# All loads of x on one queue, and a new order of tasks, in a fused state-space and MLP kernel

## The chip, the cores and the metric

One core of a Trainium2 chip runs the whole program. The metric is the device time of one execution in microseconds (us), median of several runs. The profile is one further execution; its span runs from the first to the last instruction of the program.

## The reference, cut to what matters

All inputs are bf16; L = 2048 positions, D = P = 448 channels, F = 1792 hidden channels.

```python
xn = layernorm(x)                                   # over the 448 channels
# branch A: a diagonal complex recurrence over the 2048 positions
Lam = Lambda_re + 1j * Lambda_im ; dt = exp(log_dt) ; Lam_bar = exp(dt * Lam)
Bu  = xn @ (((Lam_bar - 1) / Lam)[:, None] * (B_re + 1j * B_im)).T
h_t = Lam_bar * h_{t-1} + Bu_t
s   = 2 * real(h @ (C_re + 1j * C_im).T) + xn * Dskip
# branch B: an MLP on the same rows
y   = gelu_tanh(layernorm(xn) @ w1 + b1) @ w2 + b2
out = x + s * silu(y)
```

## The kernel before, in words

The 2048 positions are cut into 8 blocks of 256 rows; partition p of a block holds its rows 2p and 2p+1 ("par" 0 and 1). Two blocks make a group g, and there are four groups. For each group the kernel normalises the rows (twice: `xn` for branch A, `xm` for branch B), transposes them (by DMA, in group 0's branch B by TensorE), and then

- mm1 (L789): `w1` times the transposed rows, 7 steps j of two hidden tiles each, every step in a first part of 6 matmuls and a second of 8, into one of three pairs of PSUM banks; a gelu on ScalarE (L793) empties the pair into `gT`. In group 0 this is done block by block with 256 columns, later with 512;
- mm2 (L814): 14 matmuls for each block and par, into bank 5 or 6 in turn; VectorE adds `b2bc` (L817, tile `o`), which frees the bank, and a silu follows (group 0 and 3 by ScalarE's Silu, L819; group 1 and 2 by Tanh, L821, and VectorE);
- Bu (L717): 14 or 7 matmuls into bank 4, emptied into `u_sb` (L404). VectorE turns `u` by the cosines and sines in `WT`, scans (L741), and turns back into `h_sb`;
- the output part (L857, L860, L863): `h_sb` times the scaled C, plus for par 0 a matrix `M0` that stands for what lies within a row pair.

`WT` and the small per-channel columns (`cw`, `ang`) are worked out at the start on VectorE, GpSimd and ScalarE. ScalarE loads a function table five times: exp and log at the start, gelu (L428), silu and sine (L609), gelu again (L613), silu at the end.

**Who does what, and when.** Every piece of work is a task, numbered in the order in which the program makes it. `link()` finds what each task must wait for; `emit()` then issues all 628 tasks in the list `ORDER`, so each engine, and each DMA queue, runs its own tasks in the order in which they stand there. `kb.either` gives a task two engines; the list `SECOND` names the tasks that take the second. SyncE (SP) issues nearly all DMAs; an engine's DMA issue waits in that engine's queue like any other task. Tasks that the text names by number:

| tasks | what |
|---|---|
| 21; 20, 19; 47 | loads of x: block 1; block 0's par 1 and par 0; blocks 2 and 3 |
| 16, 17, 18 | loads of the rows Lambda_re, Lambda_im, log dt |
| 22, 23; 27, 28; 30, 31; 33, 34 | the four chunks of `w1`, each in two DMAs |
| 24, 29, 32, 35 | a copy of 64 rows of each `w1` chunk to the other half (L349) |
| 95, 92, 100, 98 | row statistics of block 0 par 1, par 0, block 1 par 1, par 0 (L416) |
| 108, 104, 132, 129 | normalised rows of these (L438) |
| 109, 105, 133, 130; 111, 107, 134, 131 | their transposes on TensorE (L445), and the copies of these into `xn2T` (L404) |
| 112, 113 | the columns of b1 (L589), and their copy `b1f` (L592) |
| 103; 117, 120, ..., 140 | load of the gelu table (L428); group 0's gelus; 140 is the last that block 0 needs |
| 114, 115, 116 | first mm1 parts |
| 58 to 61 | angles: range reduction on GpSimd (59), ScalarE's absolute value (60), the sine polynomial (61) |
| 44; 45, 46 | broadcasts of b2 and of D to all partitions, issued by GpSimd; D halved |
| 173 to 178 | `ra`, `rb`: arguments of the sines (L621 to L626, tile `s_w`) |
| 275, 272, 281, 278 | mm2 of group 0, banks 6, 5, 6, 5; their b2 additions are 276, 273, 282, 279, their silus 277, 274, 283, 280 |
| 179; 180 to 184; 284 | load of the silu and sine table (L609); five sines into `WT` (L635); load of the gelu table (L613) |
| 285 to 305 | mm1 and gelus of group 1; 288, 294 are the first two gelus, 298 the matmuls that take the banks of 294 |
| 330, 334, 376; 331, 335 | Bu groups, and the copies of the banks of 330 and 334 |
| 370, 371, 373, 374; 474, 475, 477, 478 | normalised rows of groups 2 and 3 for branch B (L486 on VectorE, L487 on ScalarE) |

The b2 and D broadcasts as they stand:

```python
ld("pool", b2bc[:], ..., ["b2bc"], 114688, -50, reads=["sgn3", "w1r_3"])
ld("pool", dbc[:], ..., ["dbc"], 114688, -20, reads=["b2bc"])
```

`reads` makes the DMA wait for these: b2's for the last piece of `w1` (task 34), D's for b2's landing.

Of the kernel before, what the change touches and what calls it, by code (L numbers as in the profile page):

```python
# [13 lines left out]
PINNED = -1e5  # L14
# [146 lines left out]
20 14 1 0 19 10 95 21 22 15 17 92 96 16 18 25 93 5 23 28 98 97 26 108 3 94 104 27 2 48 91 49 30 50 66 51 4 109 111 6 105 100 99 101 31 106 112 107 102  # L161
110 114 113 115 24 56 116 57 132 119 52 118 53 55 129 29 32 67 9 47 130 34 44 103 120 131 133 117 54 134 122 12 33 58 124 123 121 127 171 156 135 42
252 169 165 40 125 128 137 126 35 141 136 7 43 172 170 253 8 143 68 173 138 59 13 174 251 256 254 163 144 258 60 142 146 176 257 166 147 139 255 61
259 260 148 41 206 151 140 164 152 154 145 205 149 153 175 63 207 150 45 263 64 155 275 38 36 62 70 179 177 69 261 276 72 178 215 262 264 272 265 193
71 277 273 180 168 181 281 194 182 219 46 75 65 160 73 74 183 191 249 76 282 77 78 80 274 86 167 197 278 285 192 158 279 79 195 283 289 198 208 196
184 190 209 287 201 362 286 37 211 250 363 293 82 85 366 367 361 290 210 81 11 217 365 39 218 364 368 216 269 187 280 369 161 188 284 288 199 266 267
292 200 294 291 83 87 298 296 185 202 297 302 162 303 295 301 299 270 300 89 322 323 304 370 373 374 324 305 203 213 212 360 310 271 204 159 214 223
221 84 224 306 325 222 189 225 359 227 268 157 226 330 186 228 229 307 311 314 231 375 341 90 230 232 331 88 441 336 233 220 234 334 235 337 335 326
327 371 237 376 236 338 377 372 312 342 339 238 241 239 328 329 340 378 332 343 379 380 344 313 308 318 345 381 347 333 382 242 240 245 356 352 243
442 383 246 244 357 247 404 465 467 351 358 346 353 354 468 405 348 385 406 408 407 412 413 472 466 355 309 411 248 409 349 417 410 421 471 384 386  # L170
387 388 350 414 415 422 469 470 416 425 319 320 398 443 426 427 389 420 418 428 429 390 423 473 419 433 315 424 451 430 434 444 463 445 392 436 474
399 477 446 447 504 316 400 478 401 496 437 391 393 402 403 480 431 505 475 435 481 317 479 506 507 497 321 432 483 484 482 508 438 509 488 439 510
489 448 476 485 511 464 499 491 492 455 500 440 532 536 513 512 514 515 394 534 533 449 395 490 450 396 540 486 502 537 397 535 452 539 493 541 501
526 545 543 516 549 538 544 542 519 521 548 546 518 551 498 550 456 566 457 517 520 527 528 522 529 453 454 567 458 530 459 487 568 531 569 590 460
461 591 552 523 524 570 525 571 593 547 494 462 592 575 495 594 574 576 580 572 557 558 573 598 577 553 599 554 595 579 582 555 601 578 596 581 503
585 586 587 583 588 556 589 563 602 603 597 559 600 560 584 564 611 608 604 605 561 612 562 565 613 606 609 616 620 610 614 607 624 617 615 618 621
619 625 622 623 626 627
""".split()]
SECOND = [int(k) for k in """
46 52 54 55 56 63 65 72 77 78 79 80 84 85 89 90 107 113 131 134 159 162 164 178 185 186 189 190 191 197 223 225 227 229 243 249 250 259 261 329 346  # L180
359 360 370 373 374 393 439 444 463 464 474 475 497 500 502 503 505 507 520 524 569 592 604 607
# [17 lines left out]
def bass_recurrent_scan__ssm_conv_s5__mixer_channel_mlp__prompt_kernel(  # L199
# [18 lines left out]
    with ExitStack() as es:  # L218
# [49 lines left out]
        De = s_w.bitcast(BF)[:, 1, 3, 0:512].rearrange("p (d c) -> p d c", d=4)  # L268
        h_sb = SB("h_sb", [128, 2, 7, NK + 2])
# [33 lines left out]
        with nc.Block():  # L303
# [29 lines left out]
            for i, vec in enumerate((A_Lambda_re, A_Lambda_im, A_log_dt)):  # L333
                ld("act", vrows[i:i + 1, 64:512], dram_ap(vec, 0, [[D, 1], [1, D]]), [f"vr{i}"], 1000, 10 * PINNED)
# [17 lines left out]
            for par in range(2):  # L352
                ld("sp" if par or not 1 else "act", x_all[:, 0, par, :], dram_ap(A_x, par * D, [[2 * D, 128], [1, D]]), [f"x0p{par}"], 114688, S1)
# [12 lines left out]
            ld("pool", b2bc[:], dram_ap(B_b2, 0, [[0, 128], [1, D]]), ["b2bc"], 114688, -50, reads=["sgn3", "w1r_3"])  # L366
            ld("pool", dbc[:], dram_ap(A_Dskip, 0, [[0, 128], [1, D]]), ["dbc"], 114688, -20, reads=["b2bc"])
# [16 lines left out]
            def ln_stats(g, prio, blocks=(0, 1)):  # L384
                for b in blocks:
                    for par in range(2):
                        q = par * 2 + b
                        dve([lambda e, b=b, par=par, q=q: e.bn_stats(lnst[:, q, :], x_all[:, 2 * g + b, par, :])], [f"x{2 * g + b}"] , [f"st{q}"], 0.62, prio)
                for b in blocks:
                    for par in range(2):  # L390
                        q = par * 2 + b
                        dve(lambda e, q=q: e.bn_aggr(lnmv[:, g % 2, q, :], lnst[:, q, :]), [f"st{q}"],
                            [f"mv{g % 2}_{q}"], 0.16, prio)
# [612 lines left out]
```

## Time and profile before

| | |
|---|---|
| median of 3 runs | 155.37 us (155.31 to 155.9) |
| the profiled execution | 155.16 us, of which the span is 153.4 us |
| granted TensorE clock | 0.998 |
| busy: PE, VectorE (DVE), ScalarE (ACT), GpSimd (POOL) | 148.9, 134.0, 91.4, 32.9 us |
| first mm1 matmul, first mm2 matmul, end of the last matmul | 7.41, 20.08, 150.5 us |

PE is TensorE's matmul row, PEld its weight loads, SP the queue of SyncE. A row of the timeline gives the start, the length, the engine, the line, the operation and, in brackets, the idle time before it and what ended it; successive rows of one line are merged. The granted clock is full throughout, so a matmul's length shows the work and not the throttle.

### The profile page before, as it was taken

The page shows a single profiled execution, that of the slowest core. Times are in us where ns is not written, and L with a number is a line of the kernel's source. Part 1 is how long each engine was busy: PE and PEld are TensorE (multiplying, and loading weights), DVE is VectorE, ACT ScalarE, POOL GpSimd, SP SyncE. Part 2 cuts the span into 40 slices and gives each one's busy share as a digit, 9 for nine tenths or more (in the row PEclk, how much of TensorE's full clock was granted, in tenths as well). Part 3 has the DMA queues.
Part 4 walks back from the last instruction along what each step waited for, and adds up shares of the span by engine and source line. Part 5 has one row for each costly group of instructions (what it writes and reads, how often), then busy time and mean ns, then how long its engine had stood idle before and what let it go on. Part 6 is the DMA issues. An engine that isn't in the chain of part 4 may idle for free.

```text
span 153.4 us, 2996 instructions
## 1 busy us (share of the span) xinstructions
PE 148.9 (97%) x1138; PEld 87.6 (57%) x1138; DVE 134.0 (87%) x297; ACT 91.4 (60%) x167; POOL 32.9 (21%) x87
## 2 busy tenths in 40 slices
PE   7999999999999999999999999999999999999992
PEld 7777755454565667654443556764554666555551
DVE  2959989899998899999989998849999848999994
ACT  3598897998871479868765940026389337418010
POOL 5105648133810000020145000022500006000200
PEclk9999999999999999999999999999999999999999
DMA  4899999899889923000003061311900001001022
GB/s 133 244 308 383 225 220 140 146 260 126 154 155 170 135 93 68 0 6 0 0 0 60 4 128 60 68 60 23 142 19 0 0 4 60 0 0 60 4 83 98
DMA packets 31236, 14.73 MB, mean 96 GB/s; under 512 B 24752, under 2 KB 30774, under 8 KB 31222
## 3 DMA queue, kind: packets, MB, share of 16 engines
q1 hardware_dynamic: 30768, 14.14, 41.5%
q0 software_dynamic: 160, 0.23, 0.9%
q8 instruction: 9, 0.15, 0.4%
q10 hardware_dynamic: 294, 0.17, 0.4%
q14 instruction: 5, 0.04, 0.1%
HBM read 6.89 MB, written 1.84 MB: 57 GB/s over the span
## 4 chain that ended last, share of the span: by engine, by line
PE 96%; DVE 1%; issue 0%; DVEq 0%
PE psum L789 29%; PE psum L814 28%; PE psum L717 14%; PE psum L857 12%; PE psum L860 4%; PE psum L407 3%; PE psum L706 3%; PE psum L445 1%; PE psum L863 1%; DVE t L871 1%; DVE tmp L877 0%; PE psum L692 0%; DVEq L303 0%; PE psum L589 0%; DVE ones L306 0%
## 5 line engine op out<-in xcount | busy, mean ns | idle before, releaser
L789 PE MATMUL psum<-xn2T,w_sb 64*128 64x512 bf16 (+1 forms) x462 | 45.5, 346 | 0.4
L814 PE MATMUL psum<-w_sb,gT 128*128 128x448 bf16 x224 | 44.2, 353 | 0.0
L793 ACT ACTIVATE gT<-psum,b1f 128x512 bf16<-128x512 f32 (+1 forms) x66 | 36.6, 622 | 11.0 <-PE psum L789 10.5
L789 PEld LDWEIGHTS psum<-xn2T,w_sb 64*128 64x128 bf16 x462 | 24.2, 110 | 20.6 <-issue 2.6
L814 PEld LDWEIGHTS psum<-w_sb,gT 128*128 128x128 bf16 x224 | 21.8, 98 | 19.7 <-issue 0.2
L717 PE MATMUL psum<-xnT,BT 128*128 128x256 bf16 x196 | 24.0, 273 | 0.0
L717 PEld LDWEIGHTS psum<-xnT,BT 128*128 128x128 bf16 x196 | 18.7, 98 | 5.4 <-issue 1.1
L404 ACT ACTIVATE u_sb<-psum 128x512 bf16<-128x512 f32 (+2 forms) x21 | 9.9, 472 | 18.1 <-PE psum L717 18.0
L741 DVE TENSOR_TENSOR_SCAN s_w<-dk,vs 128x774 f32<-128x774 f32 x8 | 14.1, 1763 | 0.1
L857 PE MATMUL psum<-CZ,h_sb 128*128 128x448 bf16 x56 | 11.9, 353 | 0.0
L817 DVE TENSOR_TENSOR o<-psum,b2bc 128x448 f32<-128x448 f32 x16 | 9.6, 609 | 1.6 <-PE psum L814 1.2
L857 PE MATMUL psum<-CQ,h_sb 128*128 128x448 bf16 (+2 forms) x54 | 10.5, 332 | 0.0
L404 ACT ACTIVATE vs<-s_w 64x256 bf16<-64x256 f32 (+2 forms) x9 | 6.9, 772 | 5.5 <-DVE s_w L741 5.2
L877 POOL TENSOR_TENSOR tmp<-t,x_all 128x448 bf16<-128x448 bf16 x3 | 3.1, 1034 | 32.4 <-DVE t L871 17.8
L486 DVE TENSOR_SCALAR xn_sb<-x_all,lnw 128x448 bf16<-128x448 bf16 (+2 forms) x28 | 9.5, 368 | 0.3
L653 ACT ACTIVATE tmp<-Cr,cw 128x448 f32<-128x448 bf16 (+1 forms) x11 | 7.2, 664 | 3.2 <-DVE CQ L656 3.1
L752 POOL TENSOR_TENSOR ang<-s_w,ang 128x16 f32<-128x16 f32 x3 | 1.6, 535 | 33.6 <-ACT s_w L750 33.6
L487 ACT ACTIVATE xn_sb<-x_all,lnw 128x448 bf16<-128x448 bf16 (+2 forms) x12 | 7.4, 648 | 2.1 <-DVE xn_sb L486 2.0
L857 PEld LDWEIGHTS psum<-CZ,h_sb 128*128 128x128 bf16 x56 | 5.3, 98 | 5.1 <-DVE Cr L869 0.4
L821 ACT ACTIVATE th<-o 128x448 f32<-128x448 f32 x8 | 4.6, 573 | 5.3 <-DVE o L817 5.3
L857 PEld LDWEIGHTS psum<-CQ,h_sb 128*128 128x128 bf16 x54 | 5.1, 98 | 4.1 <-DVE tmp L877 0.4
L860 PE MATMUL psum<-M,xnT 128*128 128x448 bf16 x32 | 7.4, 352 | 0.0
(161 smaller groups left out, 195.5 us busy)
## 6 DMA issues: line engine op xcount, KB each, us to landing
out_dram<-tmp SPq DMA_DIRECT2D x7, 224.0 KB, 1.9
x_all<-in_A_x_dram SPq DMA_DIRECT2D x3, 448.0 KB, 4.3
w_sb<-in_B_w_dram SPq DMA_DIRECT2D x3, 448.0 KB, 7.3
w_sb<-in_B_w_dram SPq DMA_DIRECT2D x3, 384.0 KB, 5.7
vs<-in_A_C_re_dram SPq DMA_DIRECT2D x1, 392.0 KB, 12.2
vs<-in_A_C_im_dram SPq DMA_DIRECT2D x1, 336.0 KB, 10.4
Bn<-in_A_B_im_dram SPq DMA_DIRECT2D x1, 336.0 KB, 10.8
Bn<-in_A_B_re_dram SPq DMA_DIRECT2D x1, 336.0 KB, 10.9
```

Source lines behind the costliest of these rows:

```text
L404: kb.either(("act", [lambda e, o=o, i=i: e.activation(o, i, ACT.Copy) for o, i in pairs]), ("dve", [lambda e, o=o, i=i: e.tensor_copy(o, i ...
L486: on = [("dve", [lambda e, o=o, i=i: e.tensor_scalar(o, i, rs, nb, op0=ALU.mult, op1=ALU.add) for o, i in parts], 0.4, 0.12), ("act", [lam ...
L487: ("act", [lambda e, o=o, i=i: e.activation(o, i, ACT.Identity, bias=nb, scale=rs) for o, i in parts], 0.75, 0.2)]
L653: on = [("act", [lambda e, o=o, i=i, c=c: e.activation(tmp[o, k, :], b[i], ACT.Copy, scale=c[i]) for o, i, c in ps], 0.66 * len(ps), 0.2), ...
L717: fns = [lambda e, r=r, m=m, d=d: e.matmul(psum[:, 4, r * NK:(r + 1) * NK], BT[:, m, d, :], xnT[:, gx, d, :], start=(d == 0), stop=(d == 6 ...
L741: dve(lambda e, so=so, vi=vi: e.tensor_tensor_scan(so, dk[:].rearrange("p i c -> p (i c)"), vi, 0.0, ALU.mult, ALU.add), ["v", "vl", "dk", ...
L789: return lambda e: e.matmul(view(bk[k]), w1_sb[rows, d, fcol(2 * j + k)], rhs[rows, d, :, :], start=not second and n == 0, stop=second and ...
L793: act([lambda e, k=k: e.activation(gT[:, gb, 2 * j + k, :].rearrange("p (r c) -> p r c", r=2)[:, :, cols], view(bk[k]), ACT.Gelu_apprx_tan ...
L814: fns = [lambda e, fi=fi: e.matmul(psum[:, bk, 0:D], gT[:, gb, fi, q * 128:(q + 1) * 128], w2_sb[:, fi, :], start=(fi == 0), stop=(fi == N ...
L817: dve(lambda e: e.tensor_tensor(o2[:, fb, :], psum[:, bk, 0:D], b2bc[:], ALU.add), [f"ps{bk}", "b2bc"], [f"oo{fb}"], 0.62, prio - 76)
L857: fns = [lambda e, k=k: e.matmul(psum[:, bk, c0:c1], h_sb[:, hb, k, k0:k0 + 128], cm[:, k, c0:c1], start=(k == 0), stop=False) for k in ra ...
L860: fns += [lambda e, d=d: e.matmul(psum[:, bk, c0:c1], xnT[:, gx, d, xs], M0[:, d, c0:c1], start=False, stop=(d == 3)) for d in range(4)]
```

## The change

Four edits, with flags in the source set so that other new branches (`if 0`, `0 >> g & 1`) do nothing.

1. Block 0's par 0 (task 19) is loaded by SP and no longer by ACT, and the row log dt (task 18) too. With the new order SP issues: block 1 of x, block 0 par 1, block 0 par 0, log dt, then `w1`.
2. D's broadcast (45) waits for what b2's waits for, and no longer for b2's landing. Both stay on GpSimd's queue.
3. `ORDER` is new: all 628 tasks are there in another order.
4. `SECOND` is new. By it 19 tasks go from DVE to ACT, 12 from ACT to DVE, 26 from POOL to DVE, 18 from DVE to POOL. Among those that go to ACT are 24, 35, 46, 113, and the branch B rows 370, 373, 374, 474, 475; 164, 191, 197, 444, 477 and 500 go from ACT to DVE. No task is added or dropped, and no shape changes.

```diff
-20 14 1 0 19 10 95 21 22 15 17 92 96 16 18 25 93 5 23 28 98 97 26 108 3 94 104 27 2 48 91 49 30 50 66 51 4 109 111 6 105 100 99 101 31 106 112 107 102
...
+10 21 1 2 17 20 0 26 100 16 95 14 25 19 92 18 15 3 6 22 96 23 93 27 101 28 48 5 97 91 30 49 98 94 108 50 112 109 99 51 104 106 102 105 111 132 67 52
+53 24 107 56 110 133 114 55 54 113 129 134 66 68 115 31 4 116 29 57 11 58 130 119 118 103 171 117 131 47 169 32 9 121 170 33 120 122 59 34 60 124 43
+156 61 125 13 251 123 252 254 42 63 165 163 253 257 255 258 256 259 41 126 260 127 40 135 172 128 137 173 141 35 157 136 138 62 143 139 207 144 177
+206 205 142 158 38 148 72 175 8 146 263 140 152 145 69 147 261 149 166 70 71 151 153 44 154 7 159 262 174 275 150 36 64 155 215 45 272 46 276 264 176
+164 75 178 265 161 273 168 191 73 249 219 74 179 281 193 194 76 278 192 277 167 65 274 180 220 39 282 285 195 279 85 181 182 77 196 362 283 366 183
...
-                ld("act", vrows[i:i + 1, 64:512], dram_ap(vec, 0, [[D, 1], [1, D]]), [f"vr{i}"], 1000, 10 * PINNED)
+                ld("sp" if 1 and i == 2 else "act", vrows[i:i + 1, 64:512], dram_ap(vec, 0, [[D, 1], [1, D]]), [f"vr{i}"], 1000, 10 * PINNED)
...
-                ld("sp" if par or not 1 else "act", x_all[:, 0, par, :], dram_ap(A_x, par * D, [[2 * D, 128], [1, D]]), [f"x0p{par}"], 114688, S1)
+                ld("sp" if par or not 0 else "act", x_all[:, 0, par, :], dram_ap(A_x, par * D, [[2 * D, 128], [1, D]]), [f"x0p{par}"], 114688, S1)
...
-            ld("pool", dbc[:], dram_ap(A_Dskip, 0, [[0, 128], [1, D]]), ["dbc"], 114688, -20, reads=["b2bc"])
+            ld(("pool", "sp")[0], dbc[:], dram_ap(A_Dskip, 0, [[0, 128], [1, D]]), ["dbc"], 114688, -20, reads=[] if 0 else ["sgn3", "w1r_3"])
```

The tasks named below stand, per engine, as follows in the new order (before `|` after):

```
DVE  95 92 96 93 98 108 104 100 99 101 107 113 24  |  100 95 92 96 93 101 98 108 99 104 132 67 53 107
ACT  111 102 57 103 120 117 ...                     |  102 111 24 113 57 103 117 120 ...
ACT  155 179 261 277 180 181 182 183 191 274 197 283 184 280 284  |  155 46 179 277 274 180 181 182 283 183 184 280 284
POOL 67 9 44 12 58 7 8 68 59 13 61 45               |  58 9 59 61 13 63 158 72 8 44 7 45
PE   109 105 106 112 110 114                        |  112 109 106 105 110 133 114
```

## The prediction

> **What bounds the kernel now.** I read the page first, then the chain that ended last in order of time, then busy time by stage, then the timelines of the first 36 us and the DMA view.
>
> ```profile
> PE 148.9 (97%) x1138; PEld 87.6 (57%) x1138; DVE 134.0 (87%) x297; ACT 91.4 (60%) x167; POOL 32.9 (21%) x87
> ...
> PE 96%; DVE 1%; issue 0%; DVEq 0%
> ```
> TensorE is the bound and the chain hardly leaves it. From the first mm2 (20.08) to the last output group (149.78) it runs almost without a hole: adding each group at its quickest spacing in this trace (mm2 2.65 us, Bu 1.52 or 0.76, mm1 parts 0.645 and 0.865, output 2.08 and 1.32) gives 126.96 of these 129.70 us. Of the 2.74 us left, about 1.6 are a tenth at each change from mm1 to another kind, which any order pays; some 1.1 are real waits. So a new order can win about 1 us behind 20.08, and can lose without limit.
>
> ```profile
> 0.00:7.41 7.41, 6.22 (x66) 5.36 (x67) 4.32 (x15) 3.56 (x10) 2.83 (x14) 1.00 0.67 186
> 7.41:20.08 12.67, 12.42 (x178) 9.29 (x177) 10.55 (x41) 10.86 (x24) 5.65 (x22) 1.00 1.08 297
> 20.08:30.78 10.70, 10.70 (x58) 5.39 (x57) 9.66 (x34) 9.64 (x18) 4.82 (x15) 1.00 0.94 166
> ```
> Columns: window, length, busy PE, PEld, DVE, ACT, POOL, clock, DMA share, GB/s. In 7.41 to 20.08 PE looks busy, but its mm1 matmuls are spread (68 take 5.14 us, 76 ns each, where the first 28 take 1.65, 59 each): they wait for banks that ScalarE's gelus empty. DMA is full until 30.
>
> ```profile
> 0.79 0.86 SPq L84 DMA_DIRECT2D x_all<-in_A_x_dram  x2
> 0.80 0.41 ACTq L84 DMA_DIRECT2D x_all<-in_A_x_dram  x1
> ...
> 1.70 3.35 SPq L84 DMA_DIRECT2D w_sb<-in_B_w_dram  x6
> ...
> 3.36 1.15 DVE L416 BATCH_NORM_STATS2 lnst<-x_all 128x6 f32<-128x448 bf16 x2 [2.06 <-DMA x_all<-in_A_x_dram]
> ...
> 8.13 1.28 ACT L428 ACT_TABLE_LOAD   x1
> ...
> 12.84 0.62 POOL L84 DMA_DIRECT2D b2bc<-in_B_b_dram  x1 [4.18 <-DMA w_sb<-in_B_w_dram]
> ```
> The head is a chain: x lands, statistics, rows normalised, transposed, copied, mm1, gelu behind its table. The second place to watch is the table's return:
>
> ```profile
> 32.28 1.28 ACT L613 ACT_TABLE_LOAD   x1
> 33.66 3.58 ACT L793 ACTIVATE gT<-psum,b1f 128x512 bf16<-128x512 f32 x6
> ```
> Group 1's gelus begin at 33.66; the second (294) ends at 36.08 and the matmuls that take its banks (298) start at 36.13. There PE has no slack: what makes ScalarE late there makes the kernel late.
>
> **The change part by part.** Times are from the span's start. In the new order each task starts when its engine is through with those ahead and what it needs is there; its length is that of the row with the same line, engine and shape, and successive ones on VectorE begin some 0.07 before the last one's end, as in the rows.
>
> *Loads.* SP's issues are 0.45 apart. Block 1 goes first: alone it took 2.8 us to land, so about 3.45. Block 0 par 1 is issued at 1.24 and lands about 3.9; par 0, no longer beside it on ACT, at 1.69, about 4.3 (before: 3.34 and 3.52). The row log dt follows; it lands near 4.5, its matmuls wait until 5.4 anyway: nothing. `w1` starts 0.85 later (two more issues ahead), so chunk 0 lands at 7.1 to 7.5 instead of 6.57, and the rest 0.6 to 0.9 later: chunk 1 by 10.0, chunk 2 by 11.7, `w2` by 19.1. Their users below need them at 8.5, 10.6, 12.1 and 20.4: hidden. Uncovered, that would be the same 0.9.
>
> *Head.* VectorE now starts with block 1: statistics 3.45, 4.05, 4.6 (spacing 0.55), done 5.2; aggregates 93, 96, 101 and statistics 98 to 6.05; rows 108 to 6.45; 99 and 104 to 6.95 (before: 6.06); then block 1's rows 132, which wait for ScalarE's 102 at 7.33, to 7.8; two small ones (67, 53, from GpSimd) and the copy 107 at 8.1 to 8.5 (before 6.73 to 7.12). First mm1 at **8.55, +1.1**, at least +0.9 if block 1 lands at 3.25, +1.6 if at 3.9. On ScalarE the copies 24 and 113 (0.6 and 0.2; on VectorE 0.29 and 0.17) now stand ahead of the table load: 102 to 7.33, 111 to 7.95, 24, 113, 57 to 9.05, table to 10.4, first gelu 10.45 (before 9.51: **+0.94**). From there most is given back: gelus come every 0.72 (256 columns) or 1.15 (512), before they waited for PE 1.0 us in all (at 11.80, 13.07, 15.44, 16.53), now only twice for a little; 140 stands ahead of 147. I get 140 done at 18.5 (18.88 before) and the last mm1 part at 20.4. First mm2 **20.4, +0.3** (0 to +1.1).
>
> *VectorE to the sines.* Through 273 it gains ten small cw/ang operations (0.16 each) and 164 (0.38), and two more of 0.16 and 0.09 that stood later; it loses 24, 35, 113, 166, 193 (which now stands behind) and five small: +2.2 -2.3, nothing. It was full from 10.5 on, so it only keeps its late start less the 1.1 us that it idled for chunk 2 at 9.41: from 107's +1.35 about 0.4 is left. `rb` (178) stands behind 263, 276, 264 and 164 now: done 26.95 (25.81); 273 done 27.6 (27.23).
>
> *ScalarE to the gelu table.* Before, the sines began right behind `rb` (25.85). Now 274 stands ahead of them and needs 273: it ends 28.2. Then 180, 181, 182, 283, 183, 184, 280: 0.86+0.87+1.18+0.57+0.52+0.5+0.57 = 5.07, no longer with 191 and 197 (0.65 each, to VectorE) among them, and the table 1.28: 34.5 against 33.56, **+0.95**. PE is +0.3 there and reaches 298 with no slack, so it waits: +0.95 in all. The D row 46 stands ahead of table 179; it costs nothing if D lands by 25.2 (below).
>
> *Broadcasts.* Freeing D from b2's landing removes a wait of 0.45 us on an idle GpSimd: nothing. But b2's own issue moves behind the sine polynomial 61 (3.9 us, itself behind ScalarE's 60 at about 12): about 17.0 instead of 12.84, D's 18.0 instead of 20.98.
>
> ```profile
> b2bc<-in_B_b_dram POOLq DMA_DIRECT2D x1, 112.0 KB, 7.9
> dbc<-in_A_Dskip_dram POOLq DMA_DIRECT2D x1, 112.0 KB, 4.2
> ```
> By these two rows b2 lands between 21.2 and 24.9, D between 22.2 and 25.9. 276 needs b2 at about 23.6. b2's 7.9 was issued with 10 us of SP's transfers outstanding, D's 4.2 with 4; at 17.0 there are some 6 (Bn0 now stands behind a transpose), so I take 5.5, landing 22.5: nothing.
> The Trainium skill (DMA: Bandwidth & Descriptors, "SWDGE vs HWDGE vs iDMA") says that GpSimd's and SP's descriptors feed different internal queues of a DMA engine and that it takes them in turn. By it b2's row would hardly depend on SP's backlog, and the sum is the same; the 7.9 beside 4.2 speaks against a quick turn.
>
> *From 36 us to the tail.* Matmuls are the same. ScalarE gets branch B's rows of groups 2 and 3 (1.07 each, on VectorE 0.6) among the copies that empty bank 4. In its order 331 ends at 51.95 where 334 may start at 52.15, and 335 at 56.75 where 376 may at 56.95: hidden with 0.2 to spare; if that cover goes, each costs up to 1.07. Two g2 mm1 parts wait about 0.25 each for a gelu, mm2 of group 2 up to 0.5 for 315, the last output stage up to 0.4 for `h_sb`. Against that the 1.1 us of real waits before need not come back. I set it at 0, bounds -1.1 and +2. The tail's two last groups are swapped, the 256 columns last: +0.1.
>
> **Sum.** 0.95 + 0 + 0.1 = +1.05 us on the profiled 155.16 (span 153.4 and 1.8 around it): 156.2. The runs' median is 0.21 above that execution: **156.4**.
>
> **The rivals.** The measurement can tell about 0.5%, 0.78 us.
>
> *A, faster.* The sines are not late: the small operations that move between GpSimd and VectorE are of 0.16 to 0.6, and if VectorE comes to 273 at 26.7 or sooner (0.9 less than my list; the head at +0.9 and chunk 2 unhindered give half of it), table 284 ends by 33.6. Then PE runs from 20.4 with only the 1.6 us that all orders pay: last group 20.4+126.96+1.6 = 148.96 against 149.78, with the tail -0.7; with a head at 20.1, **-1.0: 154.4**. For it: through 273 VectorE has no more work than before, and through 284 ScalarE has none either (+2.4 -2.7). Against: 274 and 46 ahead of the sines. 0.28.
>
> *B, b2's broadcast, slower.* It lands at 24.9, 7.9 behind its issue. VectorE stands at 276 until then, everything behind it 1.3 later; 273 at 28.9, bank 5 late for 278, sines and table late: +2.3, **157.6**; +1.1 more if D's landing (25.9) holds ScalarE at 46 too. It decides from a landing at 23.6. 0.13.
>
> *C, rows on ScalarE, slower.* The 0.2 us at 334 or 376 is missed by one instruction of 1.07 and bank 4 stays full: one or both, +0.9 or +1.7 on my +1.05: **157.7** between them. For: ScalarE idled 18 us for L717 before, so there is room; against: it is room in the wrong places. 0.11.
>
> *D, it does nothing that shows.* Half of the 0.95 is not there or is earned back from the 1.1 us of waits: **155.6**. 0.14.
>
> **How the numbers follow.** Forecast 0.34, its own range 155.9 to 157.2. A quarter of it lies under 156.15, a seventh of A above 154.6. Same: 0.14 + 0.09 + 0.04 = 0.27. Faster: 0.28 - 0.04 = 0.24. Slower: 0.25 + 0.13 + 0.11 = 0.49. The range for 8 in 10 goes from A with a head at 19.9 (154.2) to B with D's landing (158.8).
>
> **What would show it.** Right: first mm1 near 8.55, first gelu 10.45, first mm2 20.4; table L613 ending at 34.5; from there PE's chain unbroken, its last matmul near 151.5. Wrong: L613 ending at 33.6 or sooner (A); VectorE idle before L817 near 24 with b2's DMA as releaser (B); PE idle before L717 with ScalarE's L404 as releaser at 50 to 60 (C); first mm1 later than 9.0, or w1's landing as releaser of L789, which I call hidden.

## The result, and the profile after

| | before | after |
|---|---|---|
| median, runs on one chip | 155.34 us (155.05 to 155.9, 4 runs) | 157.53 us (157.22 to 157.63, 4 runs) |
| the profiled execution (span) | 155.16 (153.4) | 157.51 (155.4) |

The ratio is 1.0146, 95% interval 1.0124 to 1.0167: slower by 2.2 us, where +1.05 was forecast. One kernel's runs spread here by a microsecond or two, and the moment at which TensorE reaches full speed differs between executions: ten further runs of the changed kernel (e5) had a median of 157.09. Now and then an execution falls into a slower state whatever the kernel: the medians below are of all runs, the ratios, intervals and ranges of those outside that state.

The account by TensorE's own progress, read from the timelines of both (start of the first matmul of each):

| | before | after | late by |
|---|---|---|---|
| first mm1 (114) | 7.41 | 9.06 | 1.65 |
| first mm2 (275) | 20.08 | 22.00 | 1.92 |
| 298, the first matmuls to wait for the gelu table's return | 36.13 | 38.49 | 2.36 |
| 408, an mm1 part of group 2 | 70.62 | 72.98 | 2.36 |
| 568, a Bu group of group 3 | 122.30 | 124.17 | 1.87 |
| end of the last matmul | 150.52 | 152.40 | 1.88 |

So +1.92 is lost ahead of the first mm2, +0.44 at the second gelu table, and 0.49 is won back between 408 and 568.

The page after, busy time and the chain that ended last:

```profile
PE 150.1 (97%) x1138; PEld 88.8 (57%) x1138; DVE 132.7 (85%) x292; ACT 94.9 (61%) x179; POOL 32.8 (21%) x80
...
PE 84%; ACT 6%; DVE 5%; DMA 2%; issue 1%; SPq 1%; DVEq 0%; ACTq 0%
```

The chain was 96% TensorE. Now 11% of it is ScalarE and VectorE and 2% a DMA: it leaves TensorE in the head and at the second table. Busy time by stage, the stages cut at the same tasks as before (columns as in the prediction; PEclk, the granted clock, is the number ahead of the last two):

```profile
0.00:9.06 9.06, 7.32 (x70) 6.41 (x71) 5.00 (x18) 4.57 (x14) 4.16 (x19) 1.00 0.72 206
9.06:22.00 12.94, 12.75 (x173) 9.16 (x173) 10.87 (x46) 10.79 (x24) 5.54 (x23) 1.00 1.05 285
22.00:32.70 10.70, 10.70 (x58) 5.40 (x57) 9.79 (x27) 8.43 (x16) 2.48 (x3) 1.00 0.89 178
```

The third window is 10.70 long, as before: the damage is done in the two ahead of it. The head's timeline after (in the changed source the lines stand up to nine lower, so L416 of before is L425 here):

```profile
0.81 1.34 SPq L84 DMA_DIRECT2D x_all<-in_A_x_dram  x3
...
2.58 3.35 SPq L84 DMA_DIRECT2D w_sb<-in_B_w_dram  x6
...
3.38 1.16 DVE L425 BATCH_NORM_STATS2 lnst<-x_all 128x6 f32<-128x448 bf16 x2 [2.06 <-DMA x_all<-in_A_x_dram]
...
4.73 0.63 DVE L425 BATCH_NORM_STATS2 lnst<-x_all 128x6 f32<-128x448 bf16 x1 [0.20 <-DMA x_all<-in_A_x_dram]
...
7.05 0.69 PE L416 MATMUL psum<-ones 128*128 128x128 bf16 x5
...
8.80 1.28 ACT L437 ACT_TABLE_LOAD   x1
...
11.21 1.73 ACT L802 ACTIVATE gT<-psum,b1f 128x256 bf16<-128x256 f32 x4 [1.12 <-PE psum L798]
```

Two things are new. VectorE waits for block 0 par 0, which lands at 4.71. And the five fill matmuls of one step (L416; fills are matmuls of ones whose result nobody reads, issued so that TensorE has something to do) take 0.69, where the same five took 0.44 before:

```profile
6.36 0.44 PE L407 MATMUL psum<-ones 128*128 128x128 bf16 x5
```

TensorE still runs at half speed. Its matmuls of 128 columns start 107 ns apart at first and 56 ns apart later; by this spacing it reaches full speed at 10.73, before at 6.17. The column of the granted clock, which says 1.00 in these windows, does not show it here, and so the page of before was misread too: its clock was not full throughout, but only from 6.17 on. ScalarE's table is ready at 10.09, but the first gelu starts at 11.21 because the first mm1 parts come slowly. The second table after, on ScalarE's timeline:

```profile
26.71 0.58 ACT L828 ACTIVATE g_sb<-o 128x448 bf16<-128x448 f32 x1
29.39 0.58 ACT L828 ACTIVATE g_sb<-o 128x448 bf16<-128x448 f32 x1 [2.10 <-DVE o L826]
29.87 1.70 ACT L644 ACTIVATE WT<-s_w 128x768 bf16<-128x768 f32 x2
...
34.70 1.28 ACT L622 ACT_TABLE_LOAD   x1
36.02 3.00 ACT L802 ACTIVATE gT<-psum,b1f 128x512 bf16<-128x512 f32 x5
```

ScalarE idles 2.10 us for task 273 ahead of silu 274, as the prediction said, and only then starts the sines. The broadcasts after, in the list of DMA issues:

```profile
b2bc<-in_B_b_dram POOLq DMA_DIRECT2D x1, 112.0 KB, 5.1
dbc<-in_A_Dskip_dram POOLq DMA_DIRECT2D x1, 112.0 KB, 4.9
```

### The profile page after: what moved, and what is told of

Its sections match the earlier page's. It is cut to its first block, busy times and chain, and to the rows that moved or that the text cites. A ratio compares the mean times of both kernels' runs of the same rounds, so it can differ in the third digit from the quotient of the medians.

```text
span 155.4 us, 2999 instructions
## 1 busy us (share of the span) xinstructions
PE 150.1 (97%) x1138; PEld 88.8 (57%) x1138; DVE 132.7 (85%) x292; ACT 94.9 (61%) x179; POOL 32.8 (21%) x80
## 3 DMA queue, kind: packets, MB, share of 16 engines
HBM read 6.89 MB, written 1.84 MB: 56 GB/s over the span
## 4 chain that ended last, share of the span: by engine, by line
PE 84%; ACT 6%; DVE 5%; DMA 2%; issue 1%; SPq 1%; DVEq 0%; ACTq 0%
PE psum L798 26%; PE psum L823 22%; PE psum L726 14%; PE psum L866 12%; PE psum L869 4%; PE psum L715 3%; ACT WT L644 2%; DMA x_all<-in_A_x_dram 2%; ACT gT L802 2%; PE psum L454 1%; ACT g_sb L828 1%; PE psum L872 1%; ACT L622 1%; DVE o L826 1%; DVE lnst L425 1%
## 5 line engine op out<-in xcount | busy, mean ns | idle before, releaser
L798 PE MATMUL psum<-xn2T,w_sb 64*128 64x512 bf16 (+1 forms) x462 | 46.1, 351 | 0.5 <-ACT gT L802 0.3
L413 ACT ACTIVATE u_sb<-psum 128x512 bf16<-128x512 f32 (+2 forms) x22 | 10.5, 476 | 18.5 <-PE psum L726 18.4
L496 ACT ACTIVATE xn_sb<-x_all,lnw 128x384 bf16<-128x384 bf16 (+2 forms) x20 | 11.6, 624 | 7.2 <-DVE xn_sb L495 7.1
L413 ACT ACTIVATE vs<-s_w 64x256 bf16<-64x256 f32 (+2 forms) x12 | 8.2, 680 | 7.0 <-DVE s_w L750 6.3
L842 POOL TENSOR_TENSOR xd<-xn_sb,dbc 128x448 bf16<-128x448 bf16 x4 | 5.0, 1260 | 21.2 <-DVE Cr L878 13.3
L828 ACT ACTIVATE g_sb<-o 128x448 bf16<-128x448 f32 x8 | 4.5, 571 | 5.0 <-DVE o L826 4.8
L416 PE MATMUL psum<-ones 128*128 128x128 bf16 x46 | 5.6, 311 | 1.4 <-DVE ones L307 1.4
L395 DVE BATCH_NORM_STATS2 lnst<-x_all 128x6 f32<-128x448 bf16 x12 | 7.0, 609 | 0.0
```

The costliest lines, as they stand in the source:

```text
L413: kb.either(("act", [lambda e, o=o, i=i: e.activation(o, i, ACT.Copy) for o, i in pairs]), ("dve", [lambda e, o=o, i=i: e.tensor_copy(o, i ...
L496: ("act", [lambda e, o=o, i=i: e.activation(o, i, ACT.Identity, bias=nb, scale=rs) for o, i in parts], 0.75, 0.2)]
L798: return lambda e: e.matmul(view(bk[k]), w1_sb[rows, d, fcol(2 * j + k)], rhs[rows, d, :, :], start=not second and n == 0, stop=second and ...
L828: act(lambda e: e.activation(g_sb[:, gs, :], o2[:, fb, :], ACT.Silu), [f"oo{fb}", f"Ws{g}"], [f"g{gs}"])
```

## The experiments

The question was what makes the head 1.9 us late where +0.3 was forecast. Two theories. The clock: a hole in TensorE's work ahead of the first rows leaves it at half speed for longer, and the late first mm1 parts hold the gelus. The queue: block 0 par 0, third on SyncE's queue, lands late, the whole head follows, and nothing is given back behind the first gelu. The letters in the expectations are explained where they first stand: H and R with e1, C and L with e3, F with e5, Q and X with e6. Ratios are to the kernel before, measured beside it.

### Head and rest exchanged

**e1:** the head of before and the rest of after. **e2:** the head of after and the rest of before.

```diff
 # e1, in the source of before
-ORDER: all of before
+ORDER: before's as far as the first mm2 (275), then the remaining tasks in the new order, on its engines
 # e2, in the source of after
-ORDER: all of after
+ORDER: after's as far as 275, then the remaining tasks in the old order, on its engines
```

> The order, the engines and the loads of before for every task that stands ahead of the first mm2 (task 275) in before's list; the remaining tasks in the order and on the engines of after. Theory H (the loss is all made ahead of the first mm2: 22.00 us against 20.08, while from there to the end both traces take 133.3 to 133.4): first mm2 near 20.1, total 155.4 within 0.5. Theory R (the gelu table's late return at 35.98, behind the new order of VectorE and ScalarE around the sines, is a loss of its own): the table still ends 1 us or more late and the total is 156.0 to 156.6.

> The other half: after's order, engines and loads for what stands ahead of task 275 in after's list, the rest as before. Theory H: first mm2 near 22.0, total 157.2 to 157.6. Theory R: total 156.2 to 156.7.

e1: 156.87 us, 1.0080 (1.0045 to 1.0116). e2: 156.96 us, 1.0081 (1.0048 to 1.0113). Both halves cost. In e1 the first mm2 is at 20.25, but the second gelu table ends at 35.46, 15.2 behind it (before 13.5, after 14.0). ScalarE has 261 and D's row 46 ahead of the silu table, which ends at 25.82 (before 23.29), and it idles for VectorE ahead of 261 (0.67), 274 (1.32) and 283 (0.63). D, which in e1 still waits for b2's landing, holds it for only 0.26 of that; after, where D lands at 23.15, ScalarE does not wait for it. Part of e1's delay is its own: VectorE waits 1.06 at 28.8 for a load of B_re, which it does not in after. So e1 does not price the rest of the change by itself, and the two halves together cost 3.2, more than the whole; both times lie outside what either theory gave. In e2 TensorE's and ScalarE's heads hold exactly the instructions of after, and par 0 even lands later (5.15). Yet the full clock is there from 5.77, the first gelu comes at 10.53 and the first mm2 at 21.17 instead of 22.00. So one head gives two results by the clock alone, some 0.8 us apart, and without the clock's loss it is still 1.1 us late. Which of the two comes is luck: it depends on when the clock's steps fall (last section).

### The fills

**e3:** after with seven more fill matmuls, so that TensorE has fewer holes at 4 to 6.5 us. **e4:** before with 24 fewer. **e5:** after again, unchanged.

```diff
 # e3
-            dummies(26)
+            dummies(28)
...
-            dummies(10, ["vr0"])
+            dummies(11, ["vr0"])
 # and in b1_columns, behind the columns of b1
+  + [lambda e: e.matmul(psum[:, 4, 128:256], ones[:, :], ones[:, :], start=True, stop=True) for _ in range(4)]
 # e4
-            dummies(26)
+            dummies(10)
...
-            dummies(10, ["vr0"])
+            dummies(2, ["vr0"])
```

> The changed kernel with 7 more idle-time matmuls on ones (2 behind the first 26, 1 behind the next 10, 4 behind the b1 columns), which fill the holes of TensorE between 4.0 and 6.5 us. Theory C (clock: in the changed kernel TensorE's matmuls keep the spacing of half the clock, 107 ns for 128 columns, until 10.73 us, in the one before until 6.17, because of these holes): full spacing from about 7.3, the mm1 parts ahead of the first gelu in 0.33 to 0.45 each and not 0.62 to 0.78, first gelu 10.2 (11.21 now), first mm2 near 21.0, total 156.3 to 156.7. Theory L (the loss is late rows of x and VectorE's order, and the half-speed matmuls lie beside ScalarE's table load): first gelu stays past 10.9, total 157.3 to 157.6.

> The kernel before with 10 and 2 idle-time matmuls instead of 26 and 10. Theory C: the full spacing comes only between 9 and 11 us instead of at 6.17, the first gelu at 10.3 to 10.5 instead of 9.51, total 156.0 to 156.5. Theory L: no change, 155.2 to 155.6.

> The changed kernel once more, nothing altered. Theory C in its sharper form (whether TensorE comes to full spacing ahead of mm1 or in the midst of it differs from execution to execution, because the holes leave it near the limit; the head of e2 is instruction for instruction this one's, and it reached full spacing at 5.77 us and its first mm2 at 21.17, where the profile of the changed kernel has 10.73 and 22.00): the runs fall into two groups, near 156.4 and near 157.4, 0.8 to 1.0 apart. Theory F (the changed kernel always starts at half spacing): all runs within 157.2 to 157.7.

e3: 156.74 us, 1.0082 (1.0052 to 1.0112); full speed by 6.47, first gelu 10.16, first mm2 20.79. e4: 156.56 us, 1.0074 (1.0044 to 1.0105); full speed from 9.09, first mm2 20.91. e5: 157.09 us, 1.0097 (1.0061 to 1.0132), runs from 155.99 to 158.3, spread out and neither in two groups nor in one, as the theories had it. The medians of e3 and e5 differ by only 0.35 and their intervals overlap, so the clock's price is taken from the profiles; e4 shows that the kernel before lives by its fills too. e5's profile shows it in the windows view:

```profile
4.35:7.76 3.41, 1.55 (x25) 1.28 (x25) 2.26 (x9) 1.15 (x7) 0.13 (x1) 1.00 0.98 285
7.76:11.18 3.42, 3.35 (x34) 2.64 (x32) 2.42 (x11) 3.07 (x8) 2.35 (x10) 0.50 1.02 287
```

In 4.35 to 7.76 TensorE is at full speed but works only 1.55 of 3.41 us, since par 0 landed at 5.7. In the next 3.41 us it is granted half. Here par 0 was 1.0 later than in after's profile, and the first mm2 came at 22.69. At 1.0052 or more, e3 has a loss left that fills do not reach.

### Where the head's remaining microsecond sits

**e6:** e3 with the copies 24 and 113 back on VectorE. **e7:** after with a few more fills and with block 0 ahead of block 1. **e8:** both.

```diff
 # e6, on e3
-ACT  102 111 24 113 57 103
+ACT  102 111 57 103
-DVE  ... 107 54
+DVE  ... 107 24 54 113
 # e7, on after (28 and 11 fills)
-SP   21 20 19 18
+SP   20 19 21 18
-DVE  100 95 92 96 93 101 98 108 99 104 132 67 53 107
+DVE  95 92 96 93 98 108 104 100 99 101 107 132 67 53
-PE   112 109 106 105 110 133 114 115 116
+PE   112 109 106 105 110 114 115 116 133
 # e8: e7 with e6's edit
```

> e3 (the changed kernel with its holes filled) with the copy of 64 rows of w1 (24, behind 107) and the copy of b1's columns (113) back on VectorE, so that they no longer stand ahead of the gelu table on ScalarE. Theory Q (ScalarE's queue ahead of the table sets the first gelu; from the first gelu to the first mm2 it is 10.5 to 10.8 us in all six profiles): table ends near 9.3 (10.06 in e3), first gelu near 9.6 (10.16), first mm2 near 20.2 (20.79), total 156.0 to 156.3. Theory X (late rows of block 0 set it): first gelu 10.0 to 10.2, total as e3, 156.5 to 156.8.

> The changed kernel with block 0's two loads ahead of block 1's on SP, VectorE's statistics and rows of blocks 0 and 1 in the order of before with the copy 107 right behind them, and block 1's transpose 133 behind 116; 24 and 113 stay on ScalarE; 3 more idle-time matmuls (2 and 1; the hole behind the b1 columns is gone by itself). Theory Q: first mm1 near 7.8 (8.39 in e3), but the table ends near 10.0 and the first gelu stays at 10.0 to 10.2, total as e3, 156.5 to 156.8. Theory X: first gelu near 9.5, first mm2 near 20.1, total 156.0 to 156.2.

> e7 with 24 and 113 on VectorE as well. Theory Q and X together (either alone leaves the other as the limit): first mm1 near 7.8, table ends near 9.2, first gelu near 9.5, first mm2 20.1, total 155.7 to 156.1: what is left over the kernel before is the gelu table's return in group 1, 0.45 later against the first mm2 than before. If Q alone holds, the same as e6.

e6: 156.51 us, 1.0078 (1.0048 to 1.0109). e7: 156.09 us, 1.0045 (1.0010 to 1.0080). e8: 156.29 us, 1.0069 (1.0039 to 1.0100). In e6 the table is ready at 9.64, 0.4 sooner than in e3, but the first gelu stays at 10.21: it waits for mm1, as X had it. In e7 the first gelu comes at 9.94 and the first mm2 at 20.61, between Q and X; e8 misses the 20.1 and 155.7 to 156.1 that were expected. With block 0 first on SyncE's queue par 0 lands at 3.3 and the first mm1 comes at 7.63. But in e8, whose first gelu comes at 9.36, before that of the kernel before, the first mm2 is still at 20.71. Its gelu 120 does not start right behind the first one (0.84 long) but at 10.77, because TensorE has block 1's transposes (133, 130) ahead of mm1 part 119. That the first gelu sets the first mm2 fell with this run. What all nine profiles with the head of the new order agree on is the stretch from the start of gelu 120 to the first mm2: 9.90 to 9.95 us (after, e2, e3, e5 to e8, and e11 and e14 below). In the kernels with the head of before it is 10.53 to 10.57 from the first gelu (before, e1, e4, e9, e12, e13, and 10.54 in e10 and e15, which have the loads late). In neither does anything shrink when the start is late.

### The loads alone, the copies alone

**e10:** before with edit 1 alone. **e15:** e10 with the hole filled. **e12:** before with the two copies on ScalarE.

```diff
 # e10, in the source of before; every other queue as before
-SP   20 21 22 ...
+SP   21 20 19 18 22 ...
-ACT  19 17 16 18 5 ...
+ACT  17 16 5 ...
 # e15, on e10
-            dummies(10, ["vr0"])
+            dummies(24, ["vr0"])
 # e12, in the source of before
-ACT  111 102 57 103
+ACT  111 102 24 113 57 103
-DVE  107 113 24 56
+DVE  107 56
```

> The kernel before with edit 1 alone: SyncE issues block 1, block 0 par 1, block 0 par 0, log dt and then w1, ScalarE only the two other rows; every other order is that of before. Theory, that a load behind others on SyncE's queue lands late: par 0 lands at 4.7 to 5.7 instead of 3.52, its statistics and the whole head are 1.0 to 2.0 later (first mm1 8.4 to 9.4, first gelu 10.3 to 11.0), and the run takes 156.0 to 157.0. By my forecast's own term par 0 lands at 4.3, first mm1 comes 0.4 to 0.8 later and is given back: 155.3 to 155.7. Rival, that the loads cost nothing since VectorE is full anyway: 155.3.

> e10 (the kernel before with the loads of edit 1 alone) with 14 more fill matmuls on TensorE ahead of the first rows, so that it does not idle 1.2 us at 5.1 to 6.3; the loads stay as late as in e10. Theory, that about half of e10's 2.2 us is the clock: full speed from 6.5 at the latest and no half-speed stretch behind it, first mm1 still at 8.2 to 8.4, first mm2 20.8 to 21.0, 156.1 to 156.4. Rival, that the late rows are all of it: first mm2 stays at 21.7, 157.4.

> The kernel before with two copies alone changed: 24 and 113 run on ScalarE, ahead of the first gelu table, as in the new order. By the prediction's step (a late first gelu is given back, since gelus waited for PE 1.0 us in all): the table ends 0.7 to 0.9 later (10.1 to 10.3), first mm2 at 20.1 to 20.4, 155.3 to 155.6. Theory from the runs so far, that nothing is given back and gelus follow each other without a hole: first mm2 20.6 to 20.9, 155.9 to 156.2.

e10: **157.47 us**, 1.0130 (1.0103 to 1.0158): the loads alone cost as much as the whole change, and more than even the theory's 156.0 to 157.0. VectorE's timeline in e10:

```profile
3.56 0.63 DVE L416 BATCH_NORM_STATS2 lnst<-x_all 128x6 f32<-128x448 bf16 x1 [2.26 <-DMA x_all<-in_A_x_dram]
4.50 0.63 DVE L416 BATCH_NORM_STATS2 lnst<-x_all 128x6 f32<-128x448 bf16 x1 [0.31 <-DMA x_all<-in_A_x_dram]
```

The second row is par 0's statistics, at 3.90 before; par 0 lands at 4.47 here, 2.75 behind its issue. The rows reach TensorE late, and it idles for them:

```profile
6.31 0.82 PE L445 MATMUL psum<-ident,xn_sb 128*128 128x128 bf16 x8 [1.24 <-DVE xn_sb L438]
```

The windows view of e10 has what follows from that hole:

```profile
3.80:7.22 3.42, 2.10 (x31) 1.52 (x28) 3.08 (x9) 1.64 (x7) 0.77 (x3) 1.00 0.78 236
7.22:10.63 3.41, 3.41 (x37) 2.38 (x36) 2.52 (x12) 2.11 (x5) 0.38 (x3) 0.50 1.07 311
10.63:14.00 3.37, 3.37 (x56) 2.71 (x52) 2.06 (x10) 2.50 (x7) 1.25 (x4) 1.00 1.04 367
```

Busy 2.10 of 3.42 us, then a stretch at clock 0.50, exactly over the first mm1 parts: 37 matmuls where the next stretch holds 56. First gelu 11.18, first mm2 21.72. With fills in the hole (e15) the windows read (in the first of them the fills start 107 ns apart, which is half speed, whatever the column says):

```profile
2.47:5.88 3.41, 3.35 (x32) 3.09 (x31) 1.58 (x5) 0.57 (x2) 0.88 (x3) 1.00 0.85 251
5.88:9.29 3.41, 3.38 (x55) 2.77 (x54) 3.26 (x12) 2.54 (x11) 0.64 (x3) 1.00 0.99 280
```

55 matmuls in 5.88 to 9.29, and no drop behind it. e15: 156.80 us, 1.0080 (1.0054 to 1.0105). Its loads are as late as e10's or later (par 0's statistics at 4.93), the first mm1 is at 8.44 and the first mm2 at 21.07. So of e10's 2.2 us the clock is 0.65 by these two profiles (first mm2 21.72 against 21.07; the medians differ by 0.67, with intervals that just touch), and the late rows are the rest, 1.5 by the medians: 1.0 at the first mm2, and 0.3 more by 298, which stands at 37.41.

e12: 155.47 us, 1.0018 (1.0004 to 1.0032). The copies are 0.8 us of work ahead of the table, and cost 0.2. By its time alone the run fits the range for "given back" (155.3 to 155.6). But before, ScalarE had 0.47 of idle between 102 (to 7.38) and 57 (7.85), which can take most of the copies ahead of the gelu. In e12's profile log dt's row came late and TensorE waited 0.70 for it, so the first mm2 (20.72) is no measure of the copies; the stretch from the first gelu to it is 10.53, as before, so nothing was given back there.

### The loads undone in the changed kernel

**e14:** after with edit 1 undone and block 0 ahead of block 1 on VectorE and TensorE.

```diff
-SP   21 20 19 18 22 ...
+SP   20 21 22 ...
-ACT  17 16 5 ...
+ACT  19 17 16 18 5 ...
 # DVE and PE as in e7, no fills added
```

> The changed kernel with edit 1 undone (ScalarE loads block 0 par 0 and all three rows; SyncE block 0 par 1, block 1, w1), and with VectorE and TensorE taking block 0 ahead of block 1, as before; no fills, all else of the new order kept. Theory, that the loads are the cause: par 0 lands at 3.5, first mm1 at 7.5, full clock from about 6.2, first mm2 at 20.1 to 20.5; the new order's table (+0.4) and later gain (-0.5) cancel, so 155.2 to 155.7. Rival, that the rest of the new order's head (copies and block 1's transposes ahead of gelus) costs by itself: first mm2 at 21 or later, 156.2 or more.

e14: 156.45 us, 1.0061 (1.0027 to 1.0095). The rival was right here: par 0 lands at 3.30, the full clock is there at 4.82, and the first mm1 is still at 8.65. TensorE's timeline of e14:

```profile
6.89 0.27 PE L598 MATMUL psum<-ident,dk 4*128 4x3 bf16 x4 [0.67 <-DMA dk<-in_B_b_dram]
...
7.14 0.40 PE L454 MATMUL psum<-ident,xn_sb 128*128 128x128 bf16 x4
```

The new order has the columns of b1 (112) ahead of the first transposes (109), and their row arrives at 6.89, when the first rows of block 0 have been ready since 6.20. Those rows were late themselves: block 1 landed at 5.25 in this run (4.01 before), and VectorE idled 0.76 for it, since its statistics (98) stand ahead of the rows (108). Besides, ScalarE has 102, which needs block 1's statistics, ahead of the copy 111. With early loads the next thing in the queue is late. So the loads are enough to explain the loss, but undoing them alone does not give it all back.

### The second table

**e11:** e7 with silu 274 behind the fourth sine.

```diff
-ACT  277 274 180 181 182 283 183 184 280 284
+ACT  277 180 181 182 283 183 274 184 280 284
```

> The run e7 (fills, and block 0 first) with one silu, 274, moved on ScalarE from ahead of the five sines to behind four of them, where it stood before. Theory, that 274's wait for 273 makes the second gelu table late: ScalarE no longer idles 2 us there, the table ends 13.4 to 13.5 behind the first mm2 and not 14.0 (about 34.1 with a first mm2 at 20.6), PE does not idle ahead of 298, and the run takes 155.6 where e7 takes 156.09. Rival, that the sines then wait for the arguments (178, on VectorE): the table stays at 14.0 behind the first mm2, 156.1.

e11: 156.76 us, 1.0117 (1.0086 to 1.0148). The theory fell. ScalarE's timeline of e11:

```profile
28.39 1.15 ACT L645 ACTIVATE WT<-s_w,sgn 128x1024 bf16<-128x1024 f32 x1
30.82 0.58 ACT L829 ACTIVATE g_sb<-o 128x448 bf16<-128x448 f32 x1 [1.28 <-DVE o L827]
```

The sines start 1.8 sooner than in e7 (26.65 against 28.48), and then ScalarE waits for VectorE at the next silu, 283: its b2 addition 282 starts at 30.17 in e11 and 30.19 in e7. Before, 282 started 8.34 behind the first mm2; here it is 9.6. So 274 was the wait to be seen in the trace, and behind it stood another, of 1.28, on VectorE, which in the new order has more to do ahead of 282. (In e7 itself 274 waits only 0.60; ScalarE had lost 1.03 just before, to D's landing at 24.8.)

One piece of what VectorE has more to do was overlooked: task 161, an operation on 128x3 elements just ahead of 273, which edit 4 moves there from GpSimd. It takes 1.00 in after, e7 and e11, with a GpSimd multiplication beside it, and 0.15 in e1, without one (rows in the last section). By these rows it makes 273, and so the sines, some 0.85 late, more than the 0.50 by which the table is late against the first mm2; no run leaves out this meeting alone, so that it is the whole of it is not shown.

### The gain behind 36 us

**e9:** before as far as the first Bu group (322), then the new order. **e13:** e9 with load 220 as early as in the new order. **e16:** before as far as 408, then the new order.

```diff
 # e9, in the source of before
-ORDER: all of before
+ORDER: before's as far as 322, then the remaining tasks in the new order, on its engines
 # e13, on e9
-SP   ... 167 208 ... 216 220 213 ...
+SP   ... 167 220 208 ... 216 213 ...
 # e16: as e9, cut at 408
```

> The kernel before up to task 322 (the first Bu group, at 40.8 us), and the new order and engines from there to the end. Theory, that the whole loss of the new order lies ahead of 36 us and the rest of it is better: its first mm2 and its second gelu table are those of before (20.1, 33.6), and from 298 to the last group it takes 110.3 where before takes 110.8, so 0.48 us less than before in all: 154.9. Rival, that the 0.48 came because ScalarE and VectorE had been held up and had other work left over at 36 us: nothing is gained, 155.3, or some of it is lost again, 155.6.

> e9 again (the kernel before up to 322, then the new order), with task 220, a load of x's later blocks, moved up in SyncE's queue to where the new order has it, at about 30.8 us instead of 42.9. Theory, that e9's 6 us were that load alone (VectorE idled 6.25 for it at 47): first mm2 20.1, second gelu table 33.6, from 298 to the last group 110.3 instead of 110.8, so 154.8 to 154.9. Rival, that the new order behind 322 needs more of its own head than that load: over 155.3.

> The kernel before up to task 408 (an mm1 part at 70.6 us), the new order and engines from there on. Theory, that the gain is that group 2's mm1 parts no longer wait for gelus: all is as before up to 70.6, from 408 to 616 it takes 75.83 instead of 76.31, 154.8 to 154.9. Rival, that VectorE is late with group 3's rows (eleven tasks that the new order does between 42 and 72 stand behind 408 here, some 4 us of its time): TensorE waits near 80, over 155.3.

e9: 161.49 us, 1.0394 (1.0369 to 1.0419). Its longest wait on VectorE's timeline:

```profile
47.11 0.63 DVE L388 BATCH_NORM_STATS2 lnst<-x_all 128x6 f32<-128x448 bf16 x1 [6.25 <-DMA x_all<-in_A_x_dram]
```

The statistics of later blocks stand early in the new order, their load (220) late in the old one. e13 puts the load right: 156.04 us, 1.0035 (1.0005 to 1.0064). From 408 to 568 it takes 51.19 us, exactly as after does, where before takes 51.68: so the gain is real and belongs to the order of that stretch. But TensorE waits 0.58 for a transposed `BT` near 48 us, 304 to 326 takes 13.48 instead of 12.74, and no time is gained in all. e16: 167.03 us, 1.0758 (1.0742 to 1.0775): its rival was right, by far. Rows of later groups that the new order makes between 42 and 72 us are made too late, and TensorE waits 9.7 us at 73 to 83. No version that I ran beats the kernel before.

## Why the prediction was right or wrong

**The step that failed: "From there most is given back"**, in *Head*, with its first mm2 at 20.4 (0 to +1.1 late). It was 22.00, +1.92, outside its bounds. The error of 1.60 splits at the first gelu.

- *0.76 ahead of it* (11.21 against 10.45). The forecast for the full clock was fair: e2 has 10.53 and e3 10.16. The clock was left out; the 1.00 of the granted clock in the windows of before was read as though it held from the start and for any order. In e2 and e15 it is worth 0.8 and 0.65. The Trainium skill (TensorE: Matmul & The Clock Gate, "What's actually happening") says that the clock is decided over a free-running window of about 3.4 us. e5 and e10 agree, with stretches of 3.41.
- *0.84 behind it* (10.79 to the first mm2, where the sum had 9.95). I counted before's 1.0 us of ScalarE waits in this stretch as slack that a late start could use. The runs show that it is not: the stretch has the same length in every kernel with the same order, however late it starts (counted from gelu 120 in the new order; the part ahead of it varies). With the full clock the head is 1.1 (e2) or 0.7 (e3) late and not 0.3. The reading behind it was wrong as well. The 68 matmuls with 76 ns each hardly wait for banks that gelus empty: two of group 0's seven steps are done for both blocks at once, and 20 of the 68 have 512 columns. Before, in 10.89 to 16.03 and in 9.51 to 20.08:

```profile
L789 PE MATMUL psum<-xn2T,w_sb 64*128 64x256 bf16 x48 | 3.6, 272 | 0.0
L789 PE MATMUL psum<-xn2T,w_sb 64*128 64x512 bf16 x20 | 2.7, 376 | 0.0
```
```profile
9.51:20.08 10.57, 10.43 (x147) 7.56 (x143) 9.04 (x34) 9.37 (x22) 5.27 (x19) 1.00 1.09 296
```

In this trace two matmuls of 256 columns start every 0.11 us and two of 512 every 0.22. By that the 68 need 4.8 of their 5.14, and all matmuls between the first gelu and the first mm2 some 9.3 of the 10.57 (estimates from these starts). So TensorE's own work fills most of the stretch, and the waits were those of ScalarE, which has time to spare (busy 9.37 of 10.57).

**The loads.** *Par 0 "about 4.3"*: it landed at 4.71, and between 4.47 and 5.69 in e2, e3, e5, e6, e10 and e15. That is 2.75 to 4.0 behind its issue, where on ScalarE's queue it took 2.7. That being third makes it slow is not shown: block 1 took 2.7 as third in e7, and 4.0 as second in e14. In e10 the landing was forecast within 0.2, and the loss came all the same: what was priced wrong is less the landing than what follows from it, the clock and a delay that nothing gives back. *`w1` hidden*: right; nothing in the head waits for it.

**ScalarE to the gelu table.** *Table +0.95, at 34.5, from a first mm2 at 20.4*, that is 14.1 behind it: right in size, 13.98 (before 13.48). The cause given, 274 ahead of the sines, is there, but e11 shows that it is not the only one. Task 161, which the list had as one more small operation (0.16 each), took 1.00. The prediction charged 298 with the whole 0.95 because it had TensorE only 0.3 late; with TensorE 1.92 late the table adds 0.44.

**Broadcasts.** Right: issued at 17.26 and 18.29 (17.0 and 18.0), landed at 22.39 and 23.15. Task 276 waits for its matmuls, not for b2; rival B did not come.

**From 36 us to the tail.** Set at 0 with -1.1 as its lower bound: it was -0.48. Before, two of group 2's mm1 parts of 6, at 70.62 and 73.91, take 0.88 and 0.90 to the next part, where the others take 0.65 to 0.68; after, all take 0.65 to 0.68. These are 0.49 in all: the two waits of about 0.25 that the forecast charged to the new order stood in the old one. Rival C did not come: TensorE has no wait at 334 or 376. **The tail** cost nothing, where +0.1 was forecast.

**Rivals A and D** asked for a head at 20.1 to 20.4 and fell with it. The forecast's own range, 155.9 to 157.2, ends below the result. The range for 8 in 10 (154.2 to 158.8) held it by luck: its upper part was drawn for rival B, and the head's loss fell into it.

**Left open.** What share of a 3.41 us stretch TensorE must work to get or keep its clock: 2.10 (e10) and 1.55 (e5) were too little, 3.38 (e15) was enough. With fills alone in it, a stretch with 2.69 (0.39 to 3.80 in e10) brought full speed, and one with 2.54 (0.50 to 3.91 in after, counted back from 10.73) did not; after's 3.91 to 7.32, with 3.04 and many tiny matmuls, did not either. Why a load takes 2.7 us in one run and 4.0 in another is open too, and what the second table would cost without the meeting of task 161.

## What to carry to other kernels

Before a delay in the head is written off as "given back", look for the stretch behind it that is paced by one engine: waits of another engine are no slack, and if the length does not depend on when the stretch starts, the delay goes through whole. A mean length over matmuls of different shapes is no sign of waits; take the shapes apart first. Idle TensorE ahead of its first work can cost more than its own length: in e10 a hole of 1.24 us was followed by 3.41 us at half speed, another 0.65. Fill matmuls there belong to the order of the loads and have to be re-sized with it. A wait at the head of an in-order queue can hide another behind it, so moving one instruction proves little until the next row has been read.

## What the runs showed that was not expected

- The clock moves in steps of 3.41 us that start at another phase in each execution (full speed from 3.80 in e10, 4.35 in e5, 6.17 in before), which goes with the spread of one kernel's runs, 155.99 to 158.3 in e5. The same fills fall into one stretch in e2 (2.36 to 5.77, TensorE busy 3.35, then full speed) and are split over two in after (2.54 and 3.04, still half speed); that each run's time follows its phase is not shown, since only one run of each kernel was profiled.
- A loss of clock is not a matter of the head alone: in e16, where TensorE idles 9.7 us, the record of the clock shows half speed from 77.24 to 87.48, three such steps, 4.7 us into running mm1.
- A tiny VectorE operation can take long beside GpSimd. Task 161, a 128x3 operation, takes 1.00 on VectorE while GpSimd multiplies a 128x448 tile that takes 1.95 there (the first two rows, of after; the same in e3, e5 to e8, e11 and e14). In e1, where the multiplication is done sooner, they take 0.15 and 1.03 (the last two rows). So both lose when they meet:

```profile
27.82 1.00 DVE L593 TENSOR_SCALAR ang<-ang 128x3 f32<-128x3 f32 x1
```
```profile
26.86 1.95 POOL L842 TENSOR_TENSOR xd<-xn_sb,dbc 128x448 bf16<-128x448 bf16 x1 [7.97 <-DVE cw L557]
```
```profile
24.59 1.03 POOL L833 TENSOR_TENSOR xd<-xn_sb,dbc 128x448 bf16<-128x448 bf16 x1 [0.36 <-ACT dbc L368]
27.09 0.15 DVE L584 TENSOR_SCALAR ang<-ang 128x3 f32<-128x3 f32 x1
```
